# Sinkhorn block attention followed by a bilinear feed-forward: unused matmuls ahead of S instead of between the mixes

## The chip, the cores and the metric

The kernel runs on one core of a Trainium2 chip. The metric is the device time of one execution in microseconds (us). Five runs of the kernel before gave 250.99, 251.00, 251.25, 251.25 and 251.27 us, median 251.25.

## The reference

Attention over 4 batches, 8 heads, 768 positions and head size 64, in 8 blocks of 96 positions. A small 8x8 matrix per head is made nearly doubly stochastic by five rounds of normalising, and mixes the blocks of keys and values; each block of queries then attends to one mixed block. The result feeds a bilinear feed-forward layer.

```python
P = sort_net
for _ in range(5):
    P = np.exp(P - np.max(P, axis=-1, keepdims=True))
    P = P / (np.sum(P, axis=-1, keepdims=True) + 1e-09)
    P = P / (np.sum(P, axis=-2, keepdims=True) + 1e-09)
k_sorted = np.einsum('bhij,bhjcd->bhicd', P, k_b)
v_sorted = np.einsum('bhij,bhjcd->bhicd', P, v_b)
scores = scale * np.matmul(q_b, k_sb.transpose(0, 1, 2, 4, 3))
attn = softmax(scores)
x = np.matmul(attn, v_sb)          # then heads side by side: (3072, 512)
out = ((x @ w_a) * (x @ w_b)) @ w_out
```

Here softmax stands for the three lines of the reference that subtract the maximum, exponentiate and divide by the sum.

## The kernel before

**Stages.** Heads are worked on in pairs, four pairs to a batch. Batch 0 is cut into two half batches (four of the eight blocks each), so that the feed-forward layer can start early; the later batches are done whole, and their attention is interleaved with the feed-forward matmuls of the batch before. Everything up to about 22 us of the span is preparation and the first half batch; the change lies there.

**Order.** The order of TensorE, GpSimd and SyncE is the order of the program text, and in this first part that of ScalarE and VectorE too (the two manual schedules at lines 402 and 403). TensorE thus takes its matmuls strictly as they are written, and a matmul that waits holds up all that stand behind it.

**The normalising (lines 411 to 441).** In each of five iterations ScalarE exponentiates (line 412), and VectorE sums, inverts and multiplies, by rows and then by columns (lines 424 to 441). TensorE has little to do: in iterations 3 and 4 it transposes the queries of two pairs each (half_q, lines 414 to 418, the matmuls are at line 176), and ScalarE copies them out. In iterations 1 to 4 it also does a tiny matmul of the row sums (line 427), which makes it wait for them, and then some unused matmuls: keep_busy (line 165) multiplies a block of zeros, warm, by itself, 128x512 columns unless told otherwise, into a tile that nobody reads. Before the loop there are eight of them (line 410).

**S.** The finished matrix is spread over columns by matmuls (to_columns, line 451) and by VectorE (spread, line 153) into s_all, called S below: the right-hand side of all mixes.

**The first half batch (lines 465 to 498).** For each pair: half_mix of the keys and of the values, 12 matmuls each (line 192), copied out by ScalarE or VectorE; half_scores, 8 matmuls (line 207), then the exponential on ScalarE (line 211); half_v, 4 transposes of the mixed values (line 219); half_o, 8 matmuls (line 242), then the reciprocal and the product on VectorE (lines 246 and 248, into xph); half_x, 4 transposes (line 233), copied into xT. These steps of the four pairs are written out in an order that lets one pair's copies run beside another pair's matmuls. half_mix has two arguments for unused matmuls that stand right ahead of its own, in the same PSUM tile: fill, how many, and cols, how wide. After this the feed-forward matmuls (line 343) begin.

**Buffers and loads.** PSUM tiles come from psA (two of two banks, for scores and outputs) and psF (four of one bank, for mixes, transposes and feed-forward products). All loads of keys, values, queries and weights are issued by GpSimd in program order.

The softmax here doesn't subtract the row's maximum and nothing guards it: scores larger than these inputs give would overflow.

## Time and profile before

| What | Value |
|---|---|
| median of five runs | 251.25 us |
| the profiled execution | 251.0 us, of which 249.2 us are its span |
| TensorE matmuls busy | 238.8 us, 96% of the span, 2330 instructions |
| TensorE weight loads busy | 139.8 us |
| VectorE busy | 112.6 us |
| ScalarE busy | 102.8 us |
| GpSimd busy | 59.4 us |
| unused matmuls into heat (line 167) | 20 recorded, from 1.3 to 11.1 us |
| unused matmuls into mixh (line 167) | 5, from 11.9 to 18.9 us |

The span runs from the first to the last instruction of the profiled execution, and start times in the profile are counted from its begin. PE stands for TensorE's matmuls, PEld for its weight loads, DVE for VectorE, ACT for ScalarE, POOL for GpSimd. In rows of forty digits each digit is one fortieth of the span, in tenths of busy time; PEclk is the clock that the throttle granted to TensorE. Matmuls are pipelined: the time from the start of one to the start of the next is what a stream of them costs, and it is shorter than the duration of one. A few matmul records are missing from the trace. In a row of a timeline the two numbers are start and duration in us, "xN" counts instructions, and brackets hold the idle time before and what ended it; "issue" is idle time for which the profile shows no cause.

### The profile page before, as it was taken

The page shows a single profiled execution, that of the slowest core. Times are in us where ns is not written, and L with a number is a line of the kernel's source. Part 1 is how long each engine was busy: PE and PEld are TensorE (multiplying, and loading weights), DVE is VectorE, ACT ScalarE, POOL GpSimd, SP SyncE. Part 2 cuts the span into 40 slices and gives each one's busy share as a digit, 9 for nine tenths or more (in the row PEclk, how much of TensorE's full clock was granted, in tenths as well). Part 3 has the DMA queues.
Part 4 walks back from the last instruction along what each step waited for, and adds up shares of the span by engine and source line. Part 5 has one row for each costly group of instructions (what it writes and reads, how often), then busy time and mean ns, then how long its engine had stood idle before and what let it go on. Part 6 is the DMA issues. An engine that isn't in the chain of part 4 may idle for free.

```text
span 249.2 us, 5660 instructions
## 1 busy us (share of the span) xinstructions
PE 238.8 (96%) x2330; PEld 139.8 (56%) x2342; DVE 112.6 (45%) x267; ACT 102.8 (41%) x203; POOL 59.4 (24%) x83
## 2 busy tenths in 40 slices
PE   7789899999999999999999999999999999999994
PEld 2366566666655455666655456666645456655443
DVE  6774546655654323464633334363616144444110
ACT  3365656366633035636343046645440033333001
POOL 8974579439300002305061000000000000000000
PEclk9999999999999999999999999999999999999999
DMA  6999999999832869646475831232133310000122
GB/s 79 199 199 197 197 202 199 207 202 201 97 63 54 169 140 158 95 77 95 81 126 132 202 101 31 45 63 45 33 84 115 121 42 3 0 0 4 42 115 95
DMA packets 49162, 26.85 MB, mean 108 GB/s; under 512 B 25968, under 2 KB 46192, under 8 KB 49136
## 3 DMA queue, kind: packets, MB, share of 16 engines
q0 software_dynamic: 20944, 14.16, 39.2%
q1 hardware_dynamic: 28048, 12.27, 21.0%
q8 instruction: 18, 0.29, 0.5%
q14 instruction: 8, 0.07, 0.1%
q10 hardware_dynamic: 144, 0.07, 0.1%
HBM read 28.32 MB, written 6.29 MB: 139 GB/s over the span
## 4 chain that ended last, share of the span: by engine, by line
PE 91%; DVE 5%; ACT 1%; issue 1%; DMA 1%; DVEq 0%
PE pf L343 50%; PE po L386 24%; PE mix L292 4%; PE o_ps L242 3%; PE sc L313 2%; PE mixh L192 2%; PE po L373 1%; PE vs_ps L282 1%; PE sc L207 1%; PE vs_ps L219 1%; PE q_ps L271 1%; PE xt_ps L233 1%; DMA p_nat<-in_sort_net_dram 1%; DVE hT L364 1%; DVE xph L248 1%
## 5 line engine op out<-in xcount | busy, mean ns | idle before, releaser
L364 DVE TENSOR_TENSOR hT<-a_sb,pf 128x384 bf16<-128x384 bf16 x95 | 52.5, 553 | 73.1 <-PE pf L343 49.2
L343 PE MATMUL pf<-xT,w_a_sb 128*128 128x384 bf16 x380 | 77.9, 327 | 0.0
L343 PE MATMUL pf<-xT,w_b_sb 128*128 128x384 bf16 x380 | 77.4, 326 | 0.0
L363 ACT CAST a_sb<-pf 128x384 bf16<-128x384 f32 x95 | 45.5, 479 | 63.9 <-PE pf L343 42.6
L386 PE MATMUL po<-w_out_sb,hT 128*128 128x512 bf16 x265 | 60.5, 379 | 0.6
L343 PEld LDWEIGHTS <-w_b_sb 128*128 128x128 bf16 x384 | 37.5, 98 | 24.9 <-issue 0.3
L343 PEld LDWEIGHTS <-w_a_sb 128*128 128x128 bf16 x384 | 34.9, 98 | 22.1
L386 PEld LDWEIGHTS <-hT 128*128 128x128 bf16 x276 | 26.4, 98 | 30.2
L161 ACT COPY o_sb<-po 128x512 f32<-128x512 f32 (+1 forms) x13 | 7.5, 577 | 50.5 <-PE po L386 49.1
L163 DVE COPY o_sb<-po 128x512 f32<-128x512 f32 (+1 forms) x12 | 7.9, 658 | 42.5 <-PE po L386 37.0
L318 ACT ACTIVATE eT<-sc 96x768 bf16<-96x768 f32 x24 | 18.1, 803 | 3.2 <-PE sc L313 3.2
L248 DVE TENSOR_TENSOR xp<-o_ps,rec 96x512 bf16<-96x512 f32 x24 | 15.7, 683 | 0.2
L161 ACT CAST kT<-mix 128x384 bf16<-128x384 f32 x24 | 10.3, 482 | 7.9 <-PE mix L292 7.9
L94 POOL DMA_DIRECT2D k<-in_k_dram x16 | 11.7, 728 | 7.2 <-PE pf L343 3.3
L94 POOL DMA_DIRECT2D v<-in_v_dram x16 | 11.6, 727 | 4.2 <-PE pf L343 2.8
L242 PEld LDWEIGHTS <-eT 96*128 96x128 bf16 x256 | 10.3, 97 | 3.3 <-ACT eT L211 0.7
L550 POOL COPY gate<-kT 1x1 bf16<-1x1 bf16 x4 | 0.7, 178 | 47.4 <-ACT kT L161 47.4
L242 PE MATMUL o_ps<-vs,eT 96*128 96x65 bf16 x256 | 11.2, 193 | 0.6 <-ACT eT L211 0.6
L94 POOL DMA_DIRECT2D q<-in_q_dram x12 | 8.7, 724 | 3.2 <-DMA w_out_sb<-in_moe_w_out_dram 1.6
L257 POOL COPY qc<-q 128x768 bf16<-128x768 bf16 x8 | 6.6, 844 | 8.2 <-DMA q<-in_q_dram 8.2
L167 PE MATMUL heat<-warm 128*128 128x512 bf16 x20 | 6.7, 472 | 1.4 <-DVE warm L77 1.3
L211 ACT ACTIVATE eT<-sc 96x768 bf16<-96x768 f32 x8 | 6.5, 808 | 3.4 <-PE sc L207 3.4
(81 smaller groups left out, 162.2 us busy)
## 6 DMA issues: line engine op xcount, KB each, us to landing
out_dram<-o_sb SPq DMA_DIRECT2D x17, 256.0 KB, 2.0
k<-in_k_dram POOLq DMA_DIRECT2D x16, 192.0 KB, 6.3
v<-in_v_dram POOLq DMA_DIRECT2D x16, 192.0 KB, 6.3
q<-in_q_dram POOLq DMA_DIRECT2D x12, 192.0 KB, 7.2
w_a_sb<-in_moe_w_a_dram POOLq DMA_DIRECT2D x6, 256.0 KB, 10.9
w_b_sb<-in_moe_w_b_dram POOLq DMA_DIRECT2D x6, 256.0 KB, 10.6
w_out_sb<-in_moe_w_out_dram POOLq DMA_DIRECT2D x3, 512.0 KB, 10.2
out_dram<-o_sb SPq DMA_DIRECT2D x12, 128.0 KB, 2.4
```

Source lines behind the costliest of these rows:

```text
L94: nc.gpsimd.dma_start(out=to, in_=_ap(t, base, [[W, P], [S * D, 2], [1, W]]))
L161: nc.scalar.copy(out=out, in_=in_)
L163: nc.vector.tensor_copy(out=out, in_=in_)
L167: nc.tensor.matmul(ps[:, 0:cols], lhsT=warm[:, 0:P], rhs=warm[:, 0:cols], start=True, stop=True)
L242: nc.tensor.matmul(o_ps[:, e, i * (D + 1):(i + 1) * (D + 1)], lhsT=eT[:, hf, e, i * BLK:i * BLK + P], rhs=vs[0:BLK, i0 + i, V0 - 1 + e * ( ...
L248: nc.vector.tensor_tensor(out=_ap(xp, i0 * 2 * D, [[nxp * 2 * D, BLK], [D, 2], [2 * D, NBH], [1, D]]), in0=_ap(o_ps, 1, [[1024, BLK], [511 ...
L292: nc.tensor.matmul(mix[e * D:(e + 1) * D, c // 3, c % 3 * P:(c % 3 + 1) * P], lhsT=src2[:, e, c * D:(c + 1) * D], rhs=s_all[:, 2 * g + e], ...
L318: nc.scalar.activation(out=eT[:, hf, :, 0:HB], in_=sc[0:BLK, :, 0:HB], func=AF.Exp, scale=float(scale))
L343: nc.tensor.matmul(pf[:, 0:HW], lhsT=w_sb[:, kc, m * P:(m + 1) * P], rhs=x_cols(b, kc, t), start=(kc == 0), stop=(kc == KA - 1))
L363: nc.scalar.copy(out=a_sb, in_=pf[:, 0:HW])
L364: nc.vector.tensor_mul(out=hT[:, m, t * HW:(t + 1) * HW], in0=a_sb, in1=ab[1][:, 0:HW])
L386: nc.tensor.matmul(po, lhsT=hT[:, m, c * P:(c + 1) * P], rhs=w_out_sb[:, m, :], start=(m == 0), stop=(m == KO - 1))
```

## The change

Four edits, all to the number and width of unused matmuls. Iterations 3 and 4 of the normalising get one more each (2 to 3, and 4 to 5). The two that stand ahead of the first mix go from 256 columns to 512. The three single ones ahead of the key mixes of pairs 2 and 3 and of the value mix of pair 3 are dropped. No useful instruction, copy, load or buffer is added, removed or moved.

```diff
-                    keep_busy(heat[:, 0], (0, 4, 3, 2, 4)[it])
+                    keep_busy(heat[:, 0], (0, 4, 3, 3, 5)[it])
...
-            half_mix(0, 0, "k", "act", fill=2, cols=256)
+            half_mix(0, 0, "k", "act", fill=2)
             half_mix(0, 0, "v", "dve")
             to_columns(1)
             half_mix(0, 1, "k", "act")
...
             half_mix(0, 1, "v", "dve")
-            half_mix(0, 2, "k", "act", fill=1)
+            half_mix(0, 2, "k", "act")
             half_o(0, 0)
             half_scores(0, 1)
             half_v(0, 1)
             half_mix(0, 2, "v", "act")
-            half_mix(0, 3, "k", "act", fill=1)
+            half_mix(0, 3, "k", "act")
             half_x(0, 0, "dve")
             half_o(0, 1)
             half_scores(0, 2)
             half_v(0, 2)
-            half_mix(0, 3, "v", "act", fill=1)
+            half_mix(0, 3, "v", "act")
```

## Prediction, written before the changed kernel was run

> **What bounds the kernel now.** I read the page first, for the whole; then the chain of work that ended last, between 11 and 27 us, where the edited lines run; then the timeline of that stretch, and tables of busy time in chosen stretches.

> ```profile
> PE   7789899999999999999999999999999999999994
> PEclk9999999999999999999999999999999999999999
> q8 instruction: 18, 0.29, 0.5%
> PE 91%; DVE 5%; ACT 1%; issue 1%; DMA 1%; DVEq 0%
> ```

> TensorE carries 91% of the chain, and from 24 us on it is hardly idle, so what the first half batch gains or loses ahead of that reaches the end almost one for one. All edits lie in the first four of the 40 slices. The chain there is:

> ```profile
> 13.09 0.31 PE mixh L192 x12
> ...
> 14.31 0.32 PE mixh L167
> ...
> 16.21 0.32 PE mixh L167
> ...
> 17.36 0.23 PE sc L207 x6
> 17.60 0.90 issue
> 18.50 0.22 PE sc L207 x2
> 18.72 0.33 PE vs_ps L219 x4
> 19.05 0.22 PE mixh L167
> ...
> 20.39 0.70 DVE xph L248
> 21.09 0.05 issue
> 21.13 0.34 PE xt_ps L233 x4
> ```

> The reader should see two things. All three matmuls that the change removes (line 167, at 14.31, 16.21 and 19.05) stand on this chain, so each looks like a gain. But after the first two comes a stop of 0.90 us, in the middle of the eight score matmuls of pair 2: six run, two follow, and the profile shows no releaser. Everything turns on what ends that stop.

> **The removed matmuls.** The timeline gives start times; with the weight loads beside them:

> ```profile
> 14.24 0.39 PE L167 MATMUL mixh<-warm 128*128 128x512 bf16 x1
> 14.56 0.27 PEld L192 LDWEIGHTS <-k 128*64 128x64 bf16 x12 [0.23 <-issue]
> ```

> The next mix begins 0.32 us after the unused matmul, and so do those at 16.14 (16.46) and, within 0.01, at 18.89 (19.20). [...] The rows give 0.32 + 0.32 + 0.31 = 0.95, since the 64-column weights of a mix are loaded only afterwards, while a mix behind a mix has no such gap. I take the rows.

> **The added matmuls.** (a) Iteration 3: one more 512-column matmul, 0.22 us by the spacing of its neighbours (three end 0.82 after the first starts, one lasting 0.39). The 24 transposes behind it move from 9.19 to 9.41 and still end before TensorE's next wait is over at 10.29 (idle 0.53). Cost nothing; ScalarE's query copies slide by 0.2 and ScalarE then has nothing to do until 12.74. Without that cover: 0.22. (b) Iteration 4: the last one ends at 11.46, to_columns starts at 11.69. One more starts 0.22 behind it, at 11.30, and the place behind that is free at 11.52, 0.17 us ahead of to_columns. Cost nothing; without that cover 0.22. (c) The two ahead of the first mix grow from 256 to 512 columns. The second moves from 12.00 to 12.10; the weights of the mix follow a 512-column matmul by 0.32, so the mix starts at 12.42 and not at 12.33, where it waited for s_all (ready 12.29). Cost 0.09; bounds 0 (if weights slip in earlier) and 0.22 (both widenings shown in full).

> **How far the gain gets before the stop.** Pair 2's key mix: 14.56 + 0.09 - 0.32 = 14.33. half_o of pair 0 then wants to start at 14.65, but its exponential ends at 14.62, shifted by 0.09, plus 0.05 for the hand-over: 14.76 instead of 14.88. So of 0.23 us 0.12 is left; what is late next is ScalarE. Then the second removal: 0.12 + 0.32 = 0.44. Its followers have room: xph of pair 0 is ready by about 16.2, the exponential of pair 1 by 16.31, kT of pair 2 by 15.5, and the loads of pair 3 follow those of pair 2 on a queue moving about 200 GB/s and were in time at 16.46 and 19.20. TensorE thus reaches the stop near 17.16 instead of 17.60.

> **What ends the stop.** The DMA view shows one instruction packet on queue 8 up to 22 us: 16 KB, beginning between 16.1 and 16.2, 0.98 us long, while the 16 DMA engines are full of loads. The counts of recorded TensorE instructions are 446 up to 17.6 us and 189 up to 12.5. I read the stop as TensorE out of instructions, resumed 2.4 us after the packet began. [...] the packet comes with under 400 recorded, queue 8 shows 18 packets for some 4,700, and the stop is 0.90 us. [...] Up to the stop the instruction count is unchanged (two matmuls added, two removed), [...]. The stop then ends at about 18.50 whatever came before, is 0.90 + 0.44 = 1.34 us long, and the first 0.44 us of gain is gone. Added matmul (a) may delay the request by up to 0.22, and four instructions more ahead of S may bring it forward a little; bounds for the end -0.4 and +0.3 us, my value 0.

> **After the stop.** Without the third, pair 3's value mix starts at 18.89 and half_x of pair 1 at 19.19. But half_o of pair 2 needs the exponential that ScalarE begins only at 18.76, behind the late scores, and ends at 19.57: it starts at 19.62, not 19.69. VectorE's chain (rec, xph, then the transposes at 21.13) follows half_o: **0.07 to 0.08 us** is what is left of 0.31.

> **Sum.** Against the profiled execution (span 249.2, 251.0 with what lies around it): 0.44 gained and lost in the stop, 0.08 kept, 0 +- 0.3 for the fetch: about 250.95. The five runs fall into 250.99 to 251.00 and 251.25 to 251.27, median 251.25; I forecast 251.2.

> **Rivals.**
> *The stop moves with the matmuls* (0.2). For it: the packet begins in the very 0.1 us in which the second removed matmul starts, and a stop that is bound to an instruction's place would move with it. [...] It would keep 0.44 + 0.08 = 0.52: about 250.7.
> *The clock falls* (0.1; the other side). [...] The trace shows the slow rate at the start alone: eight 512-column matmuls take 3.42 us (0.43 apart) from 1.27, those from 5.14 run 0.22 apart. The clock column reads 1.00 in both, so matmul spacing must be read too. The least busy 3.4 us behind S are 17.60 to 21.01:

> ```profile
> 18.04:21.46 3.42, 2.53 (x47) 1.83 (x47) 2.21 (x6) 2.09 (x3) 1.80 (x3) 1.00 1.43 195
> 17.60:21.01 3.41, 2.20 (x43) 1.54 (x42) 2.22 (x7) 1.82 (x3) 1.89 (x3) 1.00 1.41 197
> ```

> TensorE is busy for 64% there, and the rate held. With a stop of 1.34 us, plus 0.09 ahead of half_o, I get 1.98/3.41 = 58%. [...] If the point from which it decides is a share between 58 and 64%, one window runs at half rate: of its 2.53 busy us as much again by half, 1.3 us, about 252.5.
> *The fetch comes later* (0.13): (a)'s 0.22 delays the request and the packet waits longer behind loads: +0.2 to +0.5, about 251.5.

> **From cases to numbers.** Likeliest 0.57: 251.2, own range 250.9 to 251.5. A difference under 0.2% (0.5 us) can't be told from no change. Half of the first rival is beyond that bound, some of the late fetch, nearly all of the clock case, and a little of the likeliest at either end: faster 0.15, same 0.63, slower 0.22. The range 250.5 to 252.0 takes in the first rival and the late fetch and leaves out the clock case and what I have not seen.

> **What would show it.** Right: the issue stop still in pair 2's scores, longer (near 1.3 us), ended near 18.5; half_o of pair 2 right after its exponential; the same distance from there to the end. First mix at 12.42: step (c). Wrong: the stop about 0.9 us long and ended near 18.1, or gone (then up to 0.5 us or more is gained), or mixes spaced twice as wide after 18 us (the clock).

## The result and the profile after

The changed kernel is slower: median 252.33 us over 21 runs against 251.25 us over 41 runs of the kernel before, ratio 1.0044 with a 95% interval of 1.0028 to 1.0059. The forecast of 251.2 us, and its range up to 252.0, were wrong. Of the 41 runs of the kernel before, three took 252.89 to 254.82 us; their clocks are not on record.

The single runs say more than the median. Each comes with its mean granted clock. Of 22 executions 3 have a clock of 0.998 or more and a median of 250.95 us. 13 lie between 0.991 and 0.993, median 252.22, and 6 at 0.985 or 0.986, median 253.37. A stretch of 3.41 us at half rate, of which the profile below has two, lowers the mean over 250 us by 0.007, two lower it by 0.014. So I read the three groups as no fall of TensorE's clock, one stretch of it, and two. Where the clock holds, the change makes no difference that three executions could show (250.95, 250.95 and 251.18 us; the kernel before has a median of 250.98 where its clock holds, see below). By the medians one stretch costs 1.27 us (single executions lost 0.92 to 1.66) and two cost 2.42.

The profiled execution is one with two (run 253.37, span 251.6). Its page, the same rows as before:

```profile
PE   7779999999998999999999999999999999999994
PEclk9995999999999999999999999999999999999999
q8 instruction: 18, 0.29, 0.5%
PE 91%; DVE 4%; ACT 2%; issue 1%; DMA 1%; DVEq 0%
```

The busy row of TensorE has hardly moved, but the fourth digit of the clock row is a 5. The chain of work there:

```profile
17.14 0.23 PE sc L207 x6
17.38 1.38 issue
18.76 0.26 PE sc L207 x2
19.02 0.54 PE vs_ps L219 x4
...
22.99 2.75 PE pf L343 x9
25.73 0.17 PE xt_ps L233 x4
25.90 0.98 PE two L343 x6
26.88 0.18 PE pf L343
```

The stop is there, again between the sixth and the seventh score of pair 2, and is 1.38 us long instead of 0.90. Behind it the four transposes of half_v take 0.54 us, where the kernel before had 0.33, and the nine feed-forward matmuls 2.75 where it had 1.48. The rows of the kernel before:

```profile
21.87 1.48 PE pf L343 x9
...
24.49 0.18 PE pf L343
```

From 25.9 on the changed kernel has the lengths of before again (0.98 and 0.18). The last row shown starts 2.39 us later than its counterpart, which stands at 24.49, and from there to the end of the span both need the same (251.6 - 26.88 and 249.2 - 24.49, 224.7 us each). So the whole loss lies ahead of it: 0.26 us because the stop ends at 18.76 and not at 18.50, the rest at half rate. The busy times in stretches of 3.41 us (busy time and count of TensorE, its weight loads, VectorE, ScalarE and GpSimd, then the clock, the DMA share and GB/s) show where it falls and comes back:

```profile
15.23:18.64 3.41, 2.15 (x60) 1.64 (x57) 2.47 (x6) 1.64 (x4) 2.53 (x3) 1.00 1.37 200
18.64:22.06 3.42, 3.26 (x45) 2.41 (x44) 1.81 (x5) 1.91 (x3) 2.11 (x3) 0.50 1.45 197
22.06:25.47 3.41, 3.41 (x21) 1.98 (x20) 1.16 (x3) 0.66 (x2) 1.61 (x3) 0.50 1.45 196
```

### The profile page after: what moved, and what is told of

It is laid out like the page before. It is cut to its first block, busy times and chain, and to the rows that moved or that the text cites. A ratio compares the mean times of both kernels' runs of the same rounds, so it can differ in the third digit from the quotient of the medians.

```text
span 251.6 us, 5658 instructions
## 1 busy us (share of the span) xinstructions
PE 241.4 (96%) x2329; PEld 141.1 (56%) x2341; DVE 113.2 (45%) x267; ACT 102.8 (41%) x203; POOL 59.4 (24%) x83
## 4 chain that ended last, share of the span: by engine, by line
PE 91%; DVE 4%; ACT 2%; issue 1%; DMA 1%; DVEq 0%
PE pf L343 50%; PE po L386 24%; PE mix L292 4%; PE o_ps L242 3%; PE sc L313 2%; PE mixh L192 1%; PE po L373 1%; PE vs_ps L219 1%; PE sc L207 1%; PE vs_ps L282 1%; PE xt_ps L233 1%; PE q_ps L271 1%; DMA p_nat<-in_sort_net_dram 1%; PE heat L167 1%; DVE hT L364 1%
## 5 line engine op out<-in xcount | busy, mean ns | idle before, releaser
L343 PE MATMUL pf<-xT,w_a_sb 128*128 128x384 bf16 x380 | 78.7, 329 | 0.0
L318 ACT ACTIVATE eT<-sc 96x768 bf16<-96x768 f32 x24 | 18.1, 803 | 3.2 <-PE sc L313 3.2
L248 DVE TENSOR_TENSOR xp<-o_ps,rec 96x512 bf16<-96x512 f32 x24 | 15.7, 683 | 0.2
L167 PE MATMUL heat<-warm 128*128 128x512 bf16 x22 | 7.3, 472 | 1.4 <-DVE warm L77 1.3
```

The lines of the kernel that those rows point to most:

```text
L167: nc.tensor.matmul(ps[:, 0:cols], lhsT=warm[:, 0:P], rhs=warm[:, 0:cols], start=True, stop=True)
L248: nc.vector.tensor_tensor(out=_ap(xp, i0 * 2 * D, [[nxp * 2 * D, BLK], [D, 2], [2 * D, NBH], [1, D]]), in0=_ap(o_ps, 1, [[1024, BLK], [511 ...
L318: nc.scalar.activation(out=eT[:, hf, :, 0:HB], in_=sc[0:BLK, :, 0:HB], func=AF.Exp, scale=float(scale))
L343: nc.tensor.matmul(pf[:, 0:HW], lhsT=w_sb[:, kc, m * P:(m + 1) * P], rhs=x_cols(b, kc, t), start=(kc == 0), stop=(kc == KA - 1))
```

## Experiments

Theory 1: the dropped matmuls thinned the stretch around the stop, and the clock falls. Theory 2: the added ones delay S or the instruction fetch. Beside these, the fetch reading of the stop (TensorE has run out of instructions) was open. Three sets of runs of the kernel before stand beside these kernels; its clock fell in 3 of 43, 1 of 63 and 0 of 9 executions, and its median where it held was 250.98 to 251.00 us.

| Kernel | ratio to before, 95% interval | clock fell | median held / fallen, us |
|---|---|---|---|
| changed | 1.0044 (1.0028 to 1.0059) | 19 of 22 | 250.95 / 252.46 |
| ahead_only | 0.9997 (0.9979 to 1.0015) | 0 of 13 | 251.04 / - |
| drop_only | 1.0068 (1.0048 to 1.0089) | 6 of 6 | - / 252.40 |
| restore_late | 1.0024 (1.0000 to 1.0049) | 4 of 14 | 250.86 / 253.47 |
| restore_early | 1.0023 (1.0001 to 1.0044) | 9 of 22 | 250.94 / 252.57 |
| thin_fill | 1.0037 (1.0012 to 1.0061) | 10 of 22 | 251.10 / 253.62 |
| free_fill | 1.0035 (1.0011 to 1.0059) | 6 of 10 | 250.87 / 252.28 |
| defer_before | 0.9965 (0.9955 to 0.9975) | 0 of 22 | 250.15 / - |
| defer_after | 0.9972 (0.9956 to 0.9988) | 5 of 22 | 249.69 / 251.74 |
| defer_free | 0.9964 (0.9951 to 0.9978) | 0 of 5 | 250.09 / - |
| defer_late | 0.9955 (0.9942 to 0.9967) | 0 of 5 | 249.84 / - |

"Fell" is a mean clock of 0.993 or less; the others have 0.998 or more.

### The two halves of the change

ahead_only is the kernel before with the additions:

```diff
-                    keep_busy(heat[:, 0], (0, 4, 3, 2, 4)[it])
+                    keep_busy(heat[:, 0], (0, 4, 3, 3, 5)[it])
...
-            half_mix(0, 0, "k", "act", fill=2, cols=256)
+            half_mix(0, 0, "k", "act", fill=2)
```

> The added unused matmuls alone: those between the mixes are kept. Theory 1 (the clock: TensorE's clock falls for one or two stretches of 3.41 us behind the stop, because the removed matmuls no longer fill the stretch around it): the clock stays at 1.000 in nearly every execution and the median is that of before, 250.9 to 251.4. Theory 2 (the added matmuls delay S or the instruction fetch, and everything behind follows): it is as slow as the changed kernel, near 252.3. The fetch reading of the stop (it stands at a fixed count of TensorE instructions, 446 recorded before it): there are four instructions more ahead of it, so the stop should come after four of pair 2's eight score matmuls instead of six, and end near 18.5 us.

drop_only is the kernel before with the removals:

```diff
-            half_mix(0, 2, "k", "act", fill=1)
+            half_mix(0, 2, "k", "act")
...
-            half_mix(0, 3, "k", "act", fill=1)
+            half_mix(0, 3, "k", "act")
...
-            half_mix(0, 3, "v", "act", fill=1)
+            half_mix(0, 3, "v", "act")
```

> The three removals alone: the unused matmuls ahead of S are as before. Theory 1 (the clock): as slow as the changed kernel or slower, 252.0 to 252.8, with a mean clock of 0.985 to 0.993 in most executions. Theory 2 (the added matmuls are to blame): as before, 250.9 to 251.3, clock 1.000. The fetch reading: four instructions fewer ahead of the stop, so all eight score matmuls of pair 2 run and the stop comes in the transposes of half_v behind them.

The additions alone change nothing (251.04, no fall in 13). The removals alone give the whole loss (252.40, a fall in 6 of 6). Theory 2 is out.

The stop went where the fetch reading had it. The timeline of ahead_only, four instructions more ahead of the stop:

```profile
17.59 0.26 PE L207 MATMUL sc<-qT,kT 64*128 64x96 bf16 x4
18.75 0.26 PE L207 MATMUL sc<-qT,kT 64*128 64x96 bf16 x4 [0.91 <-issue]
```

and that of drop_only, four fewer:

```profile
17.15 0.34 PE L207 MATMUL sc<-qT,kT 64*128 64x96 bf16 x8
18.75 0.38 PE L219 MATMUL vs_ps<-ident,vT 128*128 128x128 bf16 x4 [1.26 <-ACT eT L211]
```

Four and four in the first. In the second all eight scores run and the stop lies behind them; the profile names ScalarE's exponential as releaser, but the chain shows that this had ended at 18.35 and that the wait went on to 18.75:

```profile
17.53 0.81 ACT eT L211
18.35 0.40 issue
```

restore_early (below), which again has four more, stops after four scores as well. The stop belongs to an instruction's number, not to a piece of work.

### Which of the removed matmuls matters

restore_late and restore_early are the changed kernel with the third, or with the first two, put back:

```diff
 # restore_late
-            half_mix(0, 3, "v", "act")
+            half_mix(0, 3, "v", "act", fill=1)
...
 # restore_early
-            half_mix(0, 2, "k", "act")
+            half_mix(0, 2, "k", "act", fill=1)
...
-            half_mix(0, 3, "k", "act")
+            half_mix(0, 3, "k", "act", fill=1)
```

> The changed kernel with the third unused matmul (ahead of pair 3's value mix, behind the stop) put back. Theory 1: the stretch of 3.41 us that decided in the profiled execution of the changed kernel ended at 18.64, before this matmul runs, so in that phase the clock still falls; the matmul can only help where the stretch lies later. Clock below 1 in about half of the executions or more, median 251.5 to 252.3. Theory 2: as the changed kernel, 252.3.

> The changed kernel with the first two unused matmuls (ahead of the key mixes of pairs 2 and 3, both before the stop) put back. Theory 1: they lie in the stretch that decides, so the clock holds in most executions, median 251.0 to 251.6; TensorE reaches the stop about 0.5 to 0.6 us later than in the changed kernel and loses nothing by it. Theory 2: as the changed kernel, 252.3. The fetch reading: four instructions more, so the stop after four of the eight scores.

Each put back lowers the number of falls, from 19 of 22 to 4 of 14 and 9 of 22, and none brings it to that of before. The expectation for restore_late missed (250.99 us against 251.5 to 252.3): I took the stretch of one profiled execution for the rule and gave the third matmul about half of the executions or more; it saves more of them than the other two together, though with these counts the order of the two is not settled. Where the clock holds, neither costs anything against the changed kernel's 250.95 (three executions): 250.86 and 250.94.

### Busy time or work

thin_fill is the kernel before, with the three matmuls between the mixes cut to a 64x64 corner of the array:

```diff
-        keep_busy(mix, fill, cols)
+        if hp == 0:
+            keep_busy(mix, fill, cols)
+        for _ in range(fill if hp else 0):
+            nc.tensor.matmul(mix[0:D, 0:cols], lhsT=warm[0:D, 0:D], rhs=warm[0:D, 0:cols],
+                             start=True, stop=True)
```

> The kernel before, but the three unused matmuls between the mixes use a 64x64 corner of the array (64 partitions, 64 output rows) over the same 512 columns: TensorE is busy as long, with a quarter of the array. If the clock goes by the time TensorE is busy, it holds as before: at most one execution in ten falls, median 250.7 to 251.3. If it goes by how much of the array works, these are worth a quarter of the full ones and the clock falls in most executions, as in the kernel with the three dropped (6 of 6 below 1): median 252.0 to 252.6.

10 of 22 fell, against 1 of 63 of the kernel before beside it: more than the first forecast allows, and fewer than the second. TensorE is as long at each of the three as before (the next mix begins 0.33 us later, before 0.32):

```profile
14.15 0.40 PE L192 MATMUL mixh<-warm 64*64 64x512 bf16 x1
14.48 0.38 PE L196 MATMUL mixh<-s_all,k 128*64 128x64 bf16 x12
```

So busy time isn't what decides about the clock. The falls are fewer than the 6 of 6 without the three, so they count for something. The profiles say the same. These are the stretch of free_fill (below) after which the clock fell, at 20.01, and one of restore_late, after which it held:

```profile
16.59:20.01 3.42, 2.27 (x49) 1.62 (x46) 1.86 (x6) 1.85 (x4) 2.72 (x4) 1.00 1.37 197
```

```profile
17.46:20.87 3.41, 2.25 (x46) 1.54 (x42) 2.11 (x6) 1.68 (x3) 2.27 (x3) 1.00 1.41 197
```

Both are busy for 66%. An estimate that does part them: for each recorded matmul its columns, times its share of 128 partitions and of 128 output rows (the largest form in the trace is 128*128), summed over a stretch and divided by 8,192, the columns of sixteen 512-column matmuls (3.46 us at the spacing of 0.216 us that the trace has). Before a fall: 0.32 in the changed kernel, 0.34 in drop_only, 0.35 in free_fill. Lowest before which it held: 0.37 in thin_fill and 0.38 in restore_late. (The kernel before has 0.37 from 7.80 to 11.22, during the normalising, but only three of the four unused matmuls of iteration 4 are recorded there; the fourth makes it 0.43.) It also fits the return: the small matmuls of 18.64 to 22.06 amount to 0.33, and the clock stays down; the three stretches after which it came back from a fall have 0.46 or more. That is a line drawn through a few profiles, not a tested threshold. With the share of the partitions alone, or of the output rows alone, the same sum parts the stretches too; with the columns alone it does not (0.52 in the changed kernel before its fall, 0.51 in restore_late, where it held). Which part of the array's work counts is open, and so is whether the narrower weight loads of thin_fill matter.

free_fill puts two unused matmuls where TensorE waits anyway, into restore_late:

```diff
-    def half_x(h, hp, eng):
+    def half_x(h, hp, eng, fill=0):
...
+        if fill:
+            room = psF.tile([P, 512], FP32, tag="F", name="xt_ps")
+            keep_busy(room, fill)
+            xt_ps = room[:, 0:NBH * BLK // 2].bitcast(BF16).rearrange("p (i t) -> p i t", i=NBH)
...
-            half_x(0, 2, "act")
+            half_x(0, 2, "act", fill=2)
```

> The changed kernel with the third unused matmul put back and two more placed where TensorE waits 0.43 us for VectorE anyway, ahead of the transposes of pair 2's outputs. With the third alone the clock fell in 4 of 14 executions. If the clock is decided by TensorE's work in whatever stretch of 3.41 us holds the stop, the two fill the late part of those stretches that begin with the stop, and fewer fall: 0 to 2 of 14; they cost nothing, so where it holds the time is as with the third alone, 250.7 to 251.3. If only work ahead of the stop counts, the share stays at a quarter or more.

6 of 10 fell, so the forecast of fewer falls missed. They cost nothing where the clock held (250.87), and they did not help; against 4 of 14 the counts can't tell whether they hurt. The fall in the profile came from a stretch that ended at 20.01, ahead of both.

### The stop itself

defer_before and defer_after issue five loads later, in the kernel before and in the changed one:

```diff
-    load_ab(0)
-    load_q_half(1)
-    load_ab(1)
...
             spread(nc.vector, pc_ps, 2, 6, 0, NBH)
+            load_ab(0)
+            load_q_half(1)
+            load_ab(1)
             load_ab(2)
```

> The kernel before, with five loads that are needed late (the first two blocks of both weight matrices and the second half of the queries) issued behind the spread of S instead of ahead of the normalising. If the stop is the wait for an instruction packet that queues with these loads, the packet comes 1 us earlier or more, the stop shrinks or goes, and up to 0.9 us is gained: 250.1 to 250.7. If the packet's time does not depend on the loads queued, the stop ends near 18.5 again and the time is 250.7 to 251.3. If the weights come too late, TensorE waits at the first feed-forward matmuls behind 21.7 us: slower.

> The changed kernel with the same five loads issued later. If the stop shrinks, the stretch behind S has less idle time, and the clock should fall in far fewer executions than 19 of 22, without any unused matmul between the mixes; then the removals bring their 0.44 us and 249.8 to 250.5 is reached. If the clock goes by the unused matmuls alone and not by the stop, it still falls in most: 251.2 to 252.5.

The first instruction packet now begins between 13.7 and 13.8 us in defer_before instead of between 16.1 and 16.2, and the stop is gone from the chain (line numbers are 4 lower here):

```profile
17.14 0.25 PE o_ps L238 x8
17.39 0.28 PE sc L203 x8
17.67 0.33 PE vs_ps L215 x4
17.99 0.22 PE mixh L163
18.21 0.31 PE mixh L188 x12
```

TensorE begins these scores at 17.32 us by the timeline, where the kernel before began them at 17.30; only the stop is missing. The median is 250.15 against 251.00 us beside it, so 0.85 of the stop's 0.90 us is gained, and the clock held in all 22 (one of them took 252.10 us all the same; why is open). The stop followed the count of instructions in the kernels above, and it is gone where the packet begins 2.4 us earlier; so I read it as a wait for instructions that these loads held up. How they hold up the packet no profile shows. In defer_after the removals bring something where the clock holds, 250.15 to 249.69, 0.46 us; but the clock fell in 5 of 22. Single executions lie so far apart (249.82 to 250.63 but for that one, and 249.39 to 250.70) that the 0.46 alone is not firm; the two profiles support it, since from to_columns to the first feed-forward matmul they need 9.03 us and 8.59. The stretches without the stop are fuller (in the profile of defer_after TensorE is busy for 85% from 17.55 to 20.96), which fits that fewer fall than 19 of 22.

Two versions of defer_after were to stop these falls: defer_free has free_fill's two matmuls, defer_late only the third of the dropped ones.

```diff
 # defer_free
-            half_x(0, 2, "act")
+            half_x(0, 2, "act", fill=2)
...
 # defer_late
-            half_mix(0, 3, "v", "act")
+            half_mix(0, 3, "v", "act", fill=1)
```

> The changed kernel with the five loads issued later, and two unused matmuls where TensorE waits 0.41 us for VectorE, ahead of the transposes of pair 2's outputs (19.1 to 19.5 us there). With the later loads alone the clock fell in 5 of 22 executions, for one stretch each. If what is left of the fall comes from stretches that hold this wait, the two matmuls end it: 0 to 2 of 22, at no cost where the clock holds (249.4 to 249.9). If it comes from the mixes ahead of it, 4 to 6 of 22 fall as before.

> The changed kernel with the five loads issued later and only the third unused matmul (ahead of pair 3's value mix) put back. Without the stop it no longer stands in the shadow of a late exponential, so it costs more than the 0.08 us it cost behind the stop: up to 0.32, so 249.7 to 250.0 where the clock holds; and the clock falls in fewer executions than 5 of 22, since every stretch of 3.41 us that is thin holds it. If the matmul makes no difference to the clock, 4 to 6 of 22 fall.

None of 5 fell in either. Five executions are too few: at a rate of 5 in 22, five without a fall happen by chance about one time in four. Whether these matmuls end the falls stays open. All four kernels with later loads beat the kernel before and the changed one by their intervals; defer_late has the lowest median, 249.84, and defer_before is the one whose clock was seen to hold often enough.

## Why the prediction was wrong

**Right, by the profile after.** The added matmuls cost nothing on the path: to_columns still waits for VectorE (idle 0.26 before it), and ahead_only has the time of before. Step (c): the first mix follows to_columns by 0.73 us instead of 0.64, the 0.09 of the sum. half_o of pair 0 waits for its exponential:

```profile
14.97 0.42 PE L242 MATMUL o_ps<-vs,eT 96*128 96x65 bf16 x8 [0.18 <-ACT eT L211]
```

The stop took in the gain of the first two removals: 1.38 us long for the 1.34 of the sum, same place. That its end would not move with the removals was my estimate; no trace shows when a packet is asked for. It ended at 18.76, not 18.50, within the bounds that I gave (+0.3). That the lengths agree so well is in part luck: TensorE reached the stop at 17.38 and not at 17.16, since S came late from a slow copy on VectorE (last section), so both ends are late by about the same. Without a fall of the clock the forecast holds, as far as three executions show: 250.95 us against 250.98 of before. (The sum's 251.0 less 0.08 is 250.92, not 250.95; nothing hangs on it.) And the first rival's size fits: without the stop the medians differ by 0.46 us and the profiles by 0.44, for the 0.52 worked out.

**Wrong: the rival "the clock falls (0.1)".** The price was right for one stretch (1.3 us, measured 1.27 by the medians; that it is so close is luck, with single executions from 0.92 to 1.66), and so was the place. What failed is the step that set its chance, and with it the range that left it out. The chance of 0.1 was my estimate; no trace had shown that 1.34 us of idling leaves the clock whole. And I set a busy share of 58% against "64%, and the rate held", read from 17.60 to 21.01. But that was none of the stretches between two steps. In steps of 3.413 us from 4.39, where its clock becomes whole, these end at 18.04 and 21.46 in that execution (in the changed kernel such steps from 4.99 lead to 18.64, where its clock fell). They were fuller, with TensorE busy for 87% and 74%: this row, and the one from 18.04 in the prediction.

```profile
14.63:18.04 3.41, 2.97 (x76) 2.22 (x76) 2.37 (x7) 2.13 (x4) 2.59 (x3) 1.00 1.39 200
```

So 64% had not been seen to hold at all in the kernel before.

The runs showed:
- The clock fell after stretches with TensorE busy for 61% (drop_only), 63% (the changed kernel) and 66% (free_fill), without an idle time over 1.3 us in them.
- Busy share was the wrong measure. thin_fill has the busy time of before and fell in 10 of 22. The removals weigh more in work than in busy time, since the three have the form 128*128 and the mixes and scores around them half of that (128*64 and 64*128).
- One profile shows one position of the steps. In the kernel before the stop was cut in two by an edge at 18.04 and looked harmless; in the changed kernel one stretch held nearly all of it (15.23 to 18.64), and with the longer stop 19 of 22 executions fell.
- A fall lasts: the small matmuls of 18.64 to 22.06 (busy for 95%, at half rate) did not bring the clock back, so the profiled execution took a second stretch, and 5 others have the mean clock of two. The sum had room for one.

The rival "the fetch comes later" came in as well, but small: in the profiled execution the packet began between 16.4 and 16.5 us instead of between 16.1 and 16.2, and the stop ended 0.26 us later. The range had room for that. The added matmul (a) was not its cause: drop_only, which lacks it, stops as late (18.75).

## What to carry to other kernels

Unused matmuls that look like pure cost on the critical chain may be holding the clock (without the three, and nothing else changed, it fell in 6 of 6 executions, with them in 3 of 43 beside these): before one is dropped, sum the work of the array, not its busy time (the estimate above), over every position of a stretch of 3.41 us, and look at the granted clock of many executions, not of one. Where TensorE stops with no releaser in the profile, count its instructions: if the stop stays at the count when work is added ahead of it, look at what may hold up the instruction fetch. Here moving five loads that nobody needed yet was worth more (0.85 us) than any setting of the unused matmuls that was tried, and only with it did the removals gain anything where the clock held.

## What was not expected of the hardware

**The end of the stop comes in steps.** In six profiles with a stop it ended at 18.24 (restore_early), at 18.50 (the kernel before and restore_late) and at 18.75 or 18.76 (the changed kernel, ahead_only and drop_only), and where the clock held, the spans of the first and last group are 0.6 us apart (248.9 against 249.5). This is where the groups near 250.7, 251.0 and 251.25 us among the runs of the kernel before come from, as far as these profiles show. to_columns began at 11.50 in the first group, at 11.62 and 11.69 in the second and at 11.86 to 11.94 in the third. Why it goes in steps is not explained.

**A copy of 32x256 on VectorE took 0.28 us or 0.53 to 0.59.** The replication of S (line 445) was slow in the four profiles of the changed kernel, ahead_only, drop_only and free_fill and fast in the others, with the same instruction. That is most of what made S late in the profile after. In the changed kernel it began 0.31 us into one of GpSimd's load issues (11.27 against 10.96), in the kernel before, where it was fast, 0.72 us into one (11.35 against 10.63). Whether that is the cause was not tried.

**The clock column does not show the start.** It reads 1.00 from the first microsecond, since the trace's clock record begins only when the rate becomes whole, at 4.39 us in the kernel before and 4.99 in the changed one. For the time ahead of that, the spacing of the matmuls tells the rate: in the kernel before 0.43 us for the 512-column ones that start up to 4.23, and 0.22 for those from 5.14.
